# Sign bits of a split-float projection in four matmul passes a half instead of six (attention stage of a fused attention, routing and MLP kernel)

## Chip, cores and metric

One core of one Trainium2 chip. The metric is the device time of one launch in microseconds (us). The kernel before takes 763.55 us, the median of 3 runs (763.53 to 763.69).

## The reference

Three stages in a row. The change sits in the first.

```python
def _attn_ref(q, k, v, proj):                      # q, k, v: 2 x 8 heads x 768 x 64, proj: 64 x 6
    q_bits = (np.einsum('bhsd,dk->bhsk', q, proj) > 0).astype(np.int64)
    k_bits = (np.einsum('bhsd,dk->bhsk', k, proj) > 0).astype(np.int64)
    q_bucket = np.sum(q_bits * 2 ** np.arange(6), axis=-1)
    k_bucket = np.sum(k_bits * 2 ** np.arange(6), axis=-1)
    mask = q_bucket[:, :, :, None] == k_bucket[:, :, None, :]
    scores = np.where(mask, scale * np.matmul(q, k.transpose(0, 1, 3, 2)), -1e9)
...
    return np.matmul(softmax(scores), v)
# then: the rows go to one of 8 experts each (two matmuls with a relu), scaled by the gate,
# then x @ w_in, softplus, @ w_out
```

A bit is the sign of a dot product, so it has to be computed to nearly full float precision: one bit wrong moves a row to another bucket.

## The kernel before

**Pairs, groups, iterations.** Attention works on 8 pairs m of heads. A pair has 6 groups: head j = 0, 1 by three blocks u of 256 query rows. The loop in `run` has one iteration `it` for each group; group g is scored in iteration g, and later pieces of it follow one to four iterations on. The loop ends after iteration 43; a hand-written list orders the last groups together with the routing and the first expert.

**Order by hand.** What an iteration issues stands in three strings: one for TensorE (PE), one for ScalarE (ACT), one for VectorE (DVE). For iterations from 5 on they are

```python
    ORDER = ("S0 T0 V0 T1 S1 F V1 T2 R V2", "O X1 H0 H1 X0 H2 A", "M0 L0 M1 L1 r L2 D")
```

S0 and S1 are the scores of two blocks of 128 query rows (line 260, tile `s`, of which there are two, so S0 of an iteration overwrites S0 of the one before). M is the row maximum on DVE (line 270); two small GpSimd (POOL) instructions turn it into scale `sc` and bias `nb` (lines 271, 272), and X is the exponential on ACT (line 281) that needs them. T transposes the result, H and L split it into a high and a low part (ACT line 298, DVE line 303), V multiplies by v (line 317), O, F and r finish a group (lines 323, 339, 348 to 359; the small `rc` of line 325 is POOL's). Each engine works its own list in order. POOL has no string of its own: after M1 of an iteration it also splits a part of v (`split_v`, lines 153 and 154) and carries a trickle of constants for the routing.

**R, A, D** prepare the pair that is scored next, one step i = 0 to 5 an iteration. Steps 0 to 3 transpose a half (384 columns) of q or k (line 180); ACT writes the high part `qH` or `kH` (line 192), DVE the low part `qL` or `kL` (line 201), both as float32r. Steps 4 and 5 make the bits of one half each: R is six passes of 384 columns into one PSUM tile (line 186), A is empty, D compares with 0 and subtracts 0 or 1 by row (line 217) into `bt`. In `bt` rows 0 to 11 and 32 to 43 belong to q of the two heads, rows 64 to 75 and 96 to 107 to k, each with the bit and the bit less one. After step 5 four DMAs on SyncE's (SP) queue put rows of `bt` below `qL` and `kH` in the tiles Q2 and K2 of each head (line 157). The scores' second pass, with Q2 and K2 (76 rows), needs them, and so adds a large negative number where two bits differ.

For pairs 2 to 7 step 4 runs in iterations 9, 15, 21, 27, 33, 39 and step 5 in the next one; the pair's first scores are those of iterations 12, 18, 24, 30, 36, 42. Pair 0 is prepared ahead of the loop and pair 1 in iterations 0 and 1, by other strings.

**Constants.** `pH` and `pL` are the high and low part of the projection, laid out 128 by 128 for q and for k.

The functions as they stand:

Of the kernel before, what the change touches and what calls it, by code (L numbers as in the profile page):

```python
# [7 lines left out]
F32 = mybir.dt.float32  # L8
F32R = mybir.dt.float32r
# [4 lines left out]
ALU = mybir.AluOpType  # L14
AX = mybir.AxisListType
PSUM = bass.MemoryType.PSUM
P = 128
# [5 lines left out]
class Attention:  # L23
# [55 lines left out]
    def consts(self):  # L79
# [18 lines left out]
        nc.vector.tensor_copy(self.pH, pb)  # L98
        nc.vector.tensor_tensor(self.pL, pb, self.pH.bitcast(F32), op=ALU.subtract)


    WARM = 8

# [55 lines left out]
    def prep_pe(self, m, i, ps_of=None):  # L159
        nc, S, HS = self.nc, self.S, self.HS  # L160
        if i == 0:
            own = ("qH", "qL", "kH", "kL", "bt")
            self.prep[m] = {}
            if m == 0:

                for n, nm in zip(("PH", "PL"), "qk"):
                    t = self.p_p.tile([P, 2, S], F32R, tag=n, name=nm + "HL")
                    self.prep[m].update({nm + "H": t[:, 0], nm + "L": t[:, 1]})
                self.prep[m]["bt"] = self.p_p.tile([P, S], F32R, tag="p0", name="bt0", bufs=3)
                own = ()  # L170
            self.prep[m].update({n: self.ah_p.tile([P, S], F32R, tag=n, name=n) for n in own})
            self.dup[m] = {(n, j): self.dup_ps[m % 2].tile([P, S], F32R, tag=f"{n}{j}", name=f"{n}{j}")
                           for n in ("Q1", "K1", "Q2", "K2") for j in range(2)}
        T = self.prep[m]
        ps = ps_of() if ps_of else self.ps_m.tile([P, 512], F32, tag="m", name="ps_prep")
        if i < 4:
            nm, c = "qk"[i % 2], i // 2
            src = self.raws[m][nm]
            for t in range(self.NT // 2):
                nc.tensor.transpose(ps[:, t * P:(t + 1) * P],  # L180
                                    src[:, self.NT // 2 * c + t].rearrange("p j d -> p (j d)"), self.ident)
        else:
            c = i - 4
            ops = [(w, a, nm + x) for a, nm in enumerate("qk") for w, x in ((self.pH, "H"), (self.pL, "H"), (self.pH, "L"))]
            for n, (w, a, nm) in enumerate(ops):
                nc.tensor.matmul(ps[:, :HS], w[:, a], T[nm][:, c * HS:(c + 1) * HS], start=(n == 0), stop=(n == len(ops) - 1))
        return ps

    def prep_act(self, m, i, ps):
        if i < 4:  # L190
            nm, c, HS = "qk"[i % 2], i // 2, self.HS
            self.nc.scalar.activation(self.prep[m][nm + "H"][:, c * HS:(c + 1) * HS], ps[:, :HS], AF.Copy, scale=self.SC)

    def prep_dve(self, m, i, ps):
        nc, HS, D, NB = self.nc, self.HS, self.D, self.NB
        T, d = self.prep[m], self.dup[m]
        heads = range(1 if m == 0 else 0, 2)
        if i < 4:
            nm, c = "qk"[i % 2], i // 2
            sl = slice(c * HS, (c + 1) * HS)  # L200
            nc.vector.scalar_tensor_tensor(T[nm + "L"][:, sl], ps[:, :HS], self.SC, T[nm + "H"][:, sl].bitcast(F32),
                                           op0=ALU.mult, op1=ALU.subtract)
            if c == 1:
                for j in heads:
                    r = slice(D * j, D * j + D)
                    if nm == "q":
                        self.dcopy(d["Q1", j][0:D], T["qH"][r])
                        self.dcopy(d["Q1", j][D:2 * D], T["qH"][r])
                        self.dcopy(d["Q2", j][0:D], T["qL"][r])
                    else:  # L210
                        self.dcopy(d["K1", j][0:D], T["kH"][r])
                        self.dcopy(d["K1", j][D:2 * D], T["kL"][r])
                        self.dcopy(d["K2", j][0:D], T["kH"][r])
        else:
            c = i - 4
            sl = slice(c * HS, (c + 1) * HS)
            nc.vector.tensor_scalar(T["bt"][:, sl], ps[:, :HS], 0.0, self.sp, op0=ALU.is_gt, op1=ALU.subtract)  # L217
            if c == 1:
                for j in heads:
                    self.dcopy(d["Q2", j][D:D + 2 * NB], T["bt"][32 * j:32 * j + 2 * NB])  # L220
                    self.dcopy(d["K2", j][D:D + 2 * NB], T["bt"][64 + 32 * j:64 + 32 * j + 2 * NB])

    def head0(self, i):

# [139 lines left out]
    def run(self, aside, aside_ps, end):  # L364
# [12 lines left out]
        for i in range(6):  # L377
            ps = self.prep_pe(0, i, ps_any)
# [11 lines left out]
        for it in range(end):  # L390
            m, r = divmod(it, GP)
            aside(it)
            if r == 0 and m + 2 < NPAIR:
                self.load(m + 2)
            ok = lambda g: 0 <= g < NG
            T_, V_, F_ = it - LT, it - LV, it - LF
            pieces = []

            for i in [it + 1] if it > 4 else []:
                mm, i = divmod(GP + i, GP)  # L400
                if mm < NPAIR:
                    pieces.append((mm, i))
            ss = {}

            def do(k):
                a, n = k[0], int(k[1]) if k[1:] else None
                if a == "S" and ok(it):
                    ss[n] = self.scores(it, n)
                elif a == "M" and ok(it):
                    self.rowmax(it, n, ss[n])  # L410
                elif k == "X0" and ok(it):
                    self.expo(it, 0)
                elif k == "X1" and ok(it - 1):
                    self.expo(it - 1, 1)
                elif a == "T" and ok(T_):
                    self.tpose_pe(T_, n)
                elif a == "H" and ok(T_):
                    self.tpose_hi(T_, n)
                elif a == "L" and ok(T_):
                    self.tpose_lo(T_, n)  # L420
                elif a == "V" and ok(V_):
                    self.pv(V_, n)
                elif a == "O" and ok(F_):
                    self.fin1(F_)
                elif a == "F" and ok(F_):
                    self.fin_pe(F_, ss.get(1))
                elif a == "r" and ok(F_):
                    self.fin_dve(F_)
                elif a == "R":
                    for x in pieces:  # L430
                        pp[x] = self.prep_pe(*x)
                elif a == "A":
                    for x in pieces:
                        self.prep_act(*x, pp[x])
                elif a == "D":
                    for x in pieces:
                        self.prep_dve(*x, pp[x])

                if a == "p":
                    pp[n] = self.prep_pe(1, n, ps_any)  # L440
                elif a == "a":
                    self.prep_act(1, n, pp[n])
                elif a == "d":
                    self.prep_dve(1, n, pp[n])
                if k == "S0":
                    fresh[:] = aside_ps(it, ss.get(0))
                    trickle.extend(fresh)
                if k == "M0":
                    for x in fresh[:1]:
                        next(x)  # L450
                if k in ("M1", "L1", "r", "D") and trickle:
                    if next(trickle[0], 0) == 0:
                        trickle.pop(0)
                if k == "M1":

                    for t in {0: range(4), 1: range(4, self.NT)}.get(it, ()):
                        self.split_v(0, t)
                    if it == 1:
                        self.consts_c()
                    vm, vt = divmod(it + 4, GP)  # L460
                    if 0 < vm < NPAIR:
                        self.split_v(vm, vt)
            todo = [x.split() for x in self.FIRST.get(it, self.ORDER)]
            left = {y for x in todo for y in x}
            while left:
                k = next(x for x in todo if x and not left.intersection(after.get(x[0], ())))
                do(k[0])
                left.remove(k.pop(0))
# [1184 lines left out]
```

## Time and profile before

| | |
|---|---|
| median of 3 runs | 763.55 us (763.53 to 763.69) |
| the profiled execution, its own time | 764.64 us |
| its span, first to last instruction | 762.9 us |
| PE busy | 749.3 us (98%), 4235 matmuls |
| DVE busy | 595.8 us (78%) |
| ACT busy | 521.6 us (68%) |
| POOL busy | 226.8 us (30%) |
| granted PE clock, mean | 0.997 |

The times are device microseconds. A row of the timeline begins with the start of an instruction in us from the span's start and with its duration; in square brackets stands the idle time of the engine just before it and what ended it. Durations on one engine overlap a little (the next instruction starts while the last one drains), so the cost of an instruction in a busy stretch is the distance from its start to the next start. SPq rows are DMA issues on SP's queue.

### The profile page before, as it was taken

To read this page: it belongs to the slowest core of one execution; us is meant where nothing else is said; L and a number is where in the kernel's file an instruction comes from. 1 tells how busy PE (TensorE), PEld (TensorE's weight loads), DVE (VectorE), ACT (ScalarE), POOL (GpSimd) and SP (SyncE) were. 2 spreads that over 40 slices of the span, in tenths; PEclk is the share of its full clock that TensorE was granted. 3 is DMA by queue.
4 is the path that set the end of the run, shared out by engine and by line. 5 is a ranking of instruction groups with operands and counts; after the bars stand their busy time and mean duration, and the time that the engine had idled before them with its cause. 6 is when DMAs were issued, how large, how long until landed. Compare 5 with 4: busy or idle time off the path is not lost. (4 is left out here: it accounts for less than half of the span.)

```text
span 762.9 us, 13131 instructions
## 1 busy us (share of the span) xinstructions
PE 749.3 (98%) x4235; PEld 646.7 (85%) x4236; DVE 595.8 (78%) x894; ACT 521.6 (68%) x870; POOL 226.8 (30%) x609
## 2 busy tenths in 40 slices
PE   9999999999999999999999999999999999999996
PEld 6899999999999967888888888788888888888874
DVE  6898888989888889999999998758546755764442
ACT  5887887887879859899998899456553443533330
POOL 4654544446565546313222133300000000000222
PEclk9999999999999999999999999999999999999998
DMA  8845627546480014679973652343110311100111
GB/s 207 195 114 130 167 71 162 149 101 167 135 236 33 15 49 130 207 270 351 354 271 113 208 168 84 107 133 111 56 55 5 107 55 56 56 0 1 56 56 55
DMA packets 72602, 95.29 MB, mean 125 GB/s; under 512 B 31842, under 2 KB 48226, under 8 KB 72528
## 3 DMA queue, kind: packets, MB, share of 16 engines
q1 hardware_dynamic: 65552, 83.46, 36.7%
q0 software_dynamic: 3744, 9.45, 3.4%
q10 hardware_dynamic: 3232, 1.48, 0.8%
q8 instruction: 35, 0.57, 0.3%
q14 instruction: 39, 0.32, 0.1%
HBM read 105.18 MB, written 10.76 MB: 152 GB/s over the span
## 5 line engine op out<-in xcount | busy, mean ns | idle before, releaser
L1012 DVE TENSOR_TENSOR wL<-wr,wH 128x1024 fp32r<-128x1024 f32 (+1 forms) x137 | 160.4, 1200 | 8.4 <-ACT wH L1007 8.3
L1007 ACT CAST wH<-wr 128x1024 fp32r<-128x1024 f32 (+1 forms) x144 | 141.4, 1005 | 8.1 <-PE ps_g L1081 3.2
L1327 ACT ACTIVATE ga<-ps_f 128x512 f32<-128x512 f32 x48 | 28.8, 600 | 124.7 <-PE ps_f L1319 121.0
L270 DVE TENSOR_REDUCE mx<-s 128x1 f32<-128x768 f32 x96 | 91.5, 953 | 20.1 <-PE s L339 17.8
L281 ACT ACTIVATE p<-s,nb,sc 128x768 f32<-128x768 f32 x96 | 95.9, 999 | 15.9 <-POOL nb L272 12.3
L303 DVE TENSOR_TENSOR PL<-ps_t,PH 128x512 fp32r<-128x512 f32 x144 | 98.2, 683 | 7.1 <-ACT PH L298 6.6
L1333 DVE SCALAR_TENSOR_TENSOR gg<-ps_f,ga 128x512 f32<-128x512 f32 x48 | 33.2, 692 | 89.0 <-ACT ga L1329 88.8
L298 ACT CAST PH<-ps_t 128x512 fp32r<-128x512 f32 x144 | 83.7, 588 | 15.5 <-PE ps_t L293 13.1
L260 PE MATMUL s<-K,Q 76*128 76x384 f32 (+1 forms) x384 | 88.1, 351 | 1.4 <-ACT p L281 1.4
L293 PE MATMUL ps_t<-ident,p 128*128 128x128 f32 x576 | 86.4, 273 | 0.4 <-DVE bt L217 0.2
L317 PE MATMUL ps_o<-PH,vhl 128*128 128x256 f32 x288 | 86.7, 317 | 0.0
L1367 POOL DMA_INDIRECT out_dram<-acc,oidx x12 | 11.7, 973 | 238.5 <-DVE acc L1365 234.7
L1319 PE MATMUL ps_f<-x2H,mwH 128*128 128x512 f32 x192 | 75.8, 395 | 0.4 <-DVE w L1293 0.4
L1358 PE MATMUL ps_o<-mwL,gH 128*128 128x512 f32 x192 | 75.8, 395 | 0.0
L1358 PE MATMUL ps_o<-mwH,gH 128*128 128x512 f32 x192 | 75.8, 395 | 0.0
L1319 PE MATMUL ps_f<-x2H,mwL 128*128 128x512 f32 x192 | 75.7, 394 | 0.0
L1319 PE MATMUL ps_f<-x2L,mwH 128*128 128x512 f32 x192 | 75.7, 394 | 0.0
L1358 PE MATMUL ps_o<-mwH,gL 128*128 128x512 f32 x192 | 75.7, 394 | 0.0
L293 PEld LDWEIGHTS ps_t<-ident,p 128*128 128x128 f32 x576 | 69.3, 141 | 2.7 <-DVE bt L217 0.6
L317 PE MATMUL ps_o<-PL,vhl 128*64 128x256 f32 x288 | 68.3, 280 | 0.0
L260 PEld LDWEIGHTS s<-K,Q 76*128 76x128 f32 (+1 forms) x384 | 63.3, 190 | 2.9 <-ACT p L281 2.4
L1140 POOL DMA_INDIRECT x_dram<-y,cpi x17 | 20.9, 1229 | 128.4 <-ACT y L1135 97.7
(292 smaller groups left out, 1653.3 us busy)
## 6 DMA issues: line engine op xcount, KB each, us to landing
wr<-in_moe_w_dram SPq DMA_DIRECT2D x136, 512.0 KB
wraw<-in_moe_w_in_dram SPq DMA_DIRECT2D x16, 512.0 KB
wraw<-in_moe_w_out_dram SPq DMA_DIRECT2D x16, 512.0 KB
Q<-qH SPq DMA_DIRECT2D x28, 192.0 KB
K<-kH SPq DMA_DIRECT2D x28, 192.0 KB
rawv<-in_v_dram SPq DMA_DIRECT2D x8, 384.0 KB
x_dram<-x SPq DMA_DIRECT2D x8, 384.0 KB
rawq<-in_q_dram SPq DMA_DIRECT2D x14, 192.0 KB
```

The costliest lines, as they stand in the source:

```text
L260: self.nc.tensor.matmul(s[:, h, :HS], d[l, j][:kk, ts], d[r, j][:kk, h * HS:(h + 1) * HS], start=(a == 0), stop=(a == 1))
L270: nc.vector.tensor_reduce(mx, s[:, :, :self.HS], axis=AX.XY, op=ALU.max)
L281: self.nc.scalar.activation(e["P"][ti].rearrange("p (h c) -> p h c", h=2), s[:, :, :self.HS], AF.Exp, scale=sc, bias=nb, accum_out=e["sum" ...
L293: self.nc.tensor.transpose(ps[:, kk, t], e["P"][t][:, kt * P:(kt + 1) * P], self.ident)
L298: self.nc.scalar.copy(e["PH"][:, 2 * bk:2 * bk + 2].rearrange("p k n -> p (k n)"), e["T", bk])
L303: self.nc.vector.tensor_tensor(e["PL"][:, sl].rearrange("p k n -> p (k n)"), e["T", bk], e["PH"][:, sl].rearrange("p k n -> p (k n)").bitc ...
L317: self.nc.tensor.matmul(O[:n, :2 * P], vh[:, j, kt, :n], e[nm][:, kt], start=(kt == 0 and n == P), stop=(kt == NT - 1 and n == P))
L1007: self.nc.scalar.copy(self.wt[s, c][0][:, sl], self.raw[c][:, sl])
L1012: eng.tensor_tensor(L[:, sl], self.raw[c][:, sl], H[:, sl].bitcast(F32), op=ALU.subtract)
L1319: nc.tensor.matmul(ps, w[:, 0, sl], x[:, k], start=(k == 0 and n == 0), stop=(k == self.KD - 1 and n == 2))
L1333: nc.vector.scalar_tensor_tensor(gg, ps, 0.0, a, op0=ALU.max, op1=ALU.add)
L1358: nc.tensor.matmul(self.ops[i], a[:, sl], w[:, 1], start=(k == 0 and n == 0), stop=(k == self.CH - 1 and n == 2))
```

## The change

For pairs 2 to 7 the bits are made in another way. Two new constants `pw` hold the projection. In `pw[0]` columns 0 to 63 are the high part as before (one copy of each bit, not two), and columns 64 up are the low part, negated. `pw[1]` has the high part alone. R becomes four passes a half: `qH` and `kH` with `pw[0]`, `qL` and `kL` with `pw[1]`. Rows 0 to 63 of the PSUM tile then hold high times high plus high times low of the data, and rows 64 up hold minus the product with the projection's low part. A copies rows 64 up to a new tile `lo` (64 by 384, ACT). D is two instructions: a comparison of rows 0 to 63 with `lo` into rows 0 to 63 of `bt` (the bit), and that less one into rows 64 up. Bit and bit less one then lie in different places, so four DMAs of 12 rows become eight of 6 rows. The constants are built on POOL after M1 of iteration 3. Pairs 0 and 1 keep the six passes.

```diff
+    def consts_bits(self):
+        G, D, NB, z = self.nc.gpsimd, self.D, self.NB, self.zeros
+        self.pw = [self.e_p.tile([P, 2, P], F32R, name=f"pw{i}") for i in range(2)]
+        for w in self.pw:
+            for i in range(2):
+                G.tensor_copy(w[:, i], z)
+        for i in range(2):
+            for j in range(2):
+                sl, c = slice(D * j, D * j + D), 32 * i + NB * j
+                h, l = (x[sl, i, 64 * i + 32 * j:64 * i + 32 * j + NB].bitcast(F32) for x in (self.pH, self.pL))
+                for w in self.pw:
+                    G.tensor_copy(w[sl, i, c:c + NB], h)
+                G.tensor_scalar(self.pw[0][sl, i, c + 64:c + 64 + NB], l, -1.0, None, op0=ALU.mult)
...
# prep_pe, steps 4 and 5
-            ops = [(w, a, nm + x) for a, nm in enumerate("qk") for w, x in ((self.pH, "H"), (self.pL, "H"), (self.pH, "L"))]
+            ws = ((self.pH, "H"), (self.pL, "H"), (self.pH, "L")) if m < 2 else ((self.pw[0], "H"), (self.pw[1], "L"))
+            ops = [(w, a, nm + x) for a, nm in enumerate("qk") for w, x in ws]
...
# prep_act
+        elif m > 1:
+            self.prep[m]["lo"] = self.ah_p.tile([64, self.HS], F32, tag="lo", name="lo")
+            self.nc.scalar.copy(self.prep[m]["lo"], ps[64:P, :self.HS])
...
# prep_dve, steps 4 and 5
+                nc.vector.tensor_tensor(bt[0:64, sl], ps[0:64, :HS], T["lo"], op=ALU.is_gt)
+                nc.vector.tensor_scalar(bt[64:P, sl], bt[0:64, sl].bitcast(F32), -1.0, None, op0=ALU.add)
...
+                    for nm, rows in (("Q2", (0, 64)), ("K2", (96, 32))):
+                        for n, r in enumerate(rows):
+                            self.dcopy(d[nm, j][D + NB * n:D + NB * (n + 1)], bt[r + NB * j:r + NB * (j + 1)])
...
# run, when M1 has been issued
+                    if it == 3:
+                        self.consts_bits()
```

Three places in the order of instructions. First POOL's list from `nb` of iteration 3 to `sc` of iteration 4, before:

```order
L272 TENSOR_SCALAR nb<-mx,sc 128x1
L153 CAST vhl<-rawv 128x2x64
L154 TENSOR_TENSOR vhl<-rawv,vhl 128x2x64
L525 IOTA iota_i 128x21
L528 CAST iota_s<-iota_i 128x21
L325 TENSOR_SCALAR rc<-sum 128x2
L271 TENSOR_SCALAR sc<-mx 128x1
```

and now, from the same `nb` (the `pw` pattern of three rows comes four times in all):

```order
L303 TENSOR_SCALAR nb<-mx,sc 128x1
L107 CAST pw_537<-zeros 128x128 x2
L107 CAST pw_538<-zeros 128x128 x2
L113 CAST pw_537<-pH 64x6
L113 CAST pw_538<-pH 64x6
L114 TENSOR_SCALAR pw_537<-pL 64x6
```

Sixteen instructions have come between `nb` and `split_v`, and so ahead of `rc`, `sc` and `nb` of iteration 4. In the changed kernel lines 303, 302 and 356 are the former 272, 271 and 325.

Second DVE's list around D of iteration 9, before:

```order
L303 TENSOR_TENSOR PL<-ps_t,PH 128x512
L217 TENSOR_SCALAR bt<-ps_prep,sp 128x384
L270 TENSOR_REDUCE mx<-s 128x1
L303 TENSOR_TENSOR PL<-ps_t,PH 128x512
L270 TENSOR_REDUCE mx<-s 128x1
```

and now:

```order
L334 TENSOR_TENSOR PL<-ps_t,PH 128x512
L241 TENSOR_TENSOR bt<-ps_prep,lo 64x384
L242 TENSOR_SCALAR bt<-bt 64x384
L301 TENSOR_REDUCE mx<-s 128x1
L334 TENSOR_TENSOR PL<-ps_t,PH 128x512
```

One DVE instruction has become two, the second of which reads what the first wrote; both stand ahead of M0 of the next iteration.

Third SP's queue after iteration 10, with the bits of pair 2, before:

```order
L361 DMA x_dram<-x 768x1x128
L157 DMA Q_697<-bt 12x768
L157 DMA K_699<-bt 12x768
L157 DMA Q_698<-bt 12x768
L157 DMA K_700<-bt 12x768
L143 DMA rawq<-in_q_dram 128x6x64 x2
```

and now:

```order
L392 DMA x_dram<-x 768x1x128
L172 DMA Q_715<-bt 6x768 x2
L172 DMA K_717<-bt 6x768 x2
L172 DMA Q_716<-bt 6x768 x2
L172 DMA K_718<-bt 6x768 x2
L158 DMA rawq<-in_q_dram 128x6x64 x2
```

Q_697 and K_699 were the tiles of the pair's first head; its last DMA was the second in line and is now the fourth.

## Rows read from the trace of the kernel before

**Rows 1.** Windows: PE, PEld, DVE, ACT, POOL busy, granted clock, DMA; iterations 8 and 9.

```profile
52.35:57.27 4.92, 4.92 (x41) 4.88 (x40) 4.61 (x11) 4.23 (x10) 2.37 (x9) 1.00 0.96 258
57.27:62.91 5.64, 5.64 (x44) 5.61 (x43) 4.71 (x8) 4.48 (x9) 2.71 (x11) 1.00 0.93 220
```

**Rows 2.** Timeline of PE, passes for the bits in iteration 9.

```profile
58.20 0.34 PE L186 MATMUL ps_prep<-qH,pL 128*128 128x384 f32 x1
...
58.90 0.35 PE L186 MATMUL ps_prep<-kL,pH 128*128 128x384 f32 x1
```

**Rows 3.** Timeline of DVE, from D of iteration 9 to M1 of iteration 10.

```profile
59.75 0.61 DVE L217 TENSOR_SCALAR bt<-ps_prep,sp 128x384 fp32r<-128x384 f32 x1
...
61.68 0.69 DVE L303 TENSOR_TENSOR PL<-ps_t,PH 128x512 fp32r<-128x512 f32 x1 [0.26 <-ACT PH L298]
62.91 0.96 DVE L270 TENSOR_REDUCE mx<-s 128x1 f32<-128x768 f32 x1 [0.55 <-PE s L339]
```

**Rows 4.** Timeline of ACT, after H2 of iteration 9.

```profile
59.81 0.37 ACT L323 COPY Os<-ps_o 128x256 f32<-128x256 f32 x1 [1.00 <-PE ps_o L317]
```

**Rows 5.** Groups of instructions by form (count, busy us, mean ns), and one line's durations (min/median/max).

```profile
L201 DVE SCALAR_TENSOR_TENSOR qL<-ps_prep,qH 128x384 fp32r<-128x384 f32 x14 | 7.7, 547 | 0.0
L192 ACT ACTIVATE qH<-ps_prep 128x384 fp32r<-128x384 f32 x14 | 6.9, 496 | 0.9 <-PE ps_prep L180 0.9
...
L236 DVE CAST K<-kHL x2: 353/479/605, 8.5 to 9.9; 64x384 fp32r<-64x384 f32 x2
```

**Rows 6.** Timeline of POOL, iterations 3 to 5.

```profile
31.82 0.23 POOL L271 TENSOR_SCALAR sc<-mx 128x1 f32<-128x1 f32 x1
32.15 0.27 POOL L272 TENSOR_SCALAR nb<-mx,sc 128x1 f32<-128x1 f32 x1
...
35.52 0.29 POOL L359 COPY x<-xr 128x128 f32<-128x128 f32 x1
35.75 0.19 POOL L535 COPY iota_s<-iota_s 128x2 f32<-128x2 f32 x1
35.88 0.24 POOL L525 IOTA iota_i<- 128x128 int32 x1
```

**Rows 7.** Timeline of ACT: X0 of iteration 4, and its accumulator's read.

```profile
32.45 0.99 ACT L281 ACTIVATE p<-s,nb,sc 128x768 f32<-128x768 f32 x1
33.34 0.19 ACT L281 ACTIVATION_READ_ACCUMULATOR p<-s,nb,sc 128x1 f32 x1
```

**Rows 8.** Timeline of PE: S0 of iterations 3, 5 and 12.

```profile
25.02 0.97 PE L260 MATMUL s<-K,Q 128*128 128x384 f32 x4 [0.95 <-ACT p L281]
...
34.00 0.95 PE L260 MATMUL s<-K,Q 128*128 128x384 f32 x4
...
70.11 0.87 PE L260 MATMUL s<-K,Q 128*128 128x384 f32 x4
```

**Rows 9.** Timeline of SP's queue: bits of pair 2, first and last of four; a load of v.

```profile
66.03 0.82 SPq L157 DMA_DIRECT2D Q<-bt  x1
...
68.48 0.71 SPq L157 DMA_DIRECT2D K<-bt  x1
...
80.90 0.40 SPq L144 DMA_DIRECT2D rawv<-in_v_dram  x1
```

**Rows 10.** Windows of a quarter us (last two columns DMA share and GB/s) around the fourth DMA's data.

```profile
69.75:70.00 0.25, 0.25 (x5) 0.25 (x4) 0.25 (x1) 0.25 (x1) 0.15 (x2) 1.00 0.61 98
70.00:70.25 0.25, 0.25 (x4) 0.25 (x3) 0.21 (x3) 0.25 (x2) 0.25 (x2) 1.00 0.20 49
```

**Rows 11.** Timeline of PE ahead of the loop and at its last matmul; a window after it.

```profile
8.52 0.53 PE L186 MATMUL ps_prep<-qHL,pL 128*128 128x384 f32 x1
8.84 0.53 PE L186 MATMUL ps_prep<-qHL,pH 128*128 128x384 f32 x1
...
755.21 0.40 PE L1358 MATMUL ps_o<-mwH,gL 128*128 128x512 f32 x1
...
757.50:758.00 0.50, 0.00 (x0) 0.00 (x0) 0.00 (x0) 0.00 (x0) 0.50 (x1) 0.71 0.00 0
```

More of the change, by code (lines that the diff above doesn't have):

```diff
@@ L216, in prep_dve @@
             sl = slice(c * HS, (c + 1) * HS)
-            nc.vector.tensor_scalar(T["bt"][:, sl], ps[:, :HS], 0.0, self.sp, op0=ALU.is_gt, op1=ALU.subtract)
+            bt = T["bt"]
+            if m < 2:
+                nc.vector.tensor_scalar(bt[:, sl], ps[:, :HS], 0.0, self.sp, op0=ALU.is_gt, op1=ALU.subtract)
+            else:
+                nc.vector.tensor_tensor(bt[0:64, sl], ps[0:64, :HS], T["lo"], op=ALU.is_gt)
+                nc.vector.tensor_scalar(bt[64:P, sl], bt[0:64, sl].bitcast(F32), -1.0, None, op0=ALU.add)
             if c == 1:
                 for j in heads:
-                    self.dcopy(d["Q2", j][D:D + 2 * NB], T["bt"][32 * j:32 * j + 2 * NB])
-                    self.dcopy(d["K2", j][D:D + 2 * NB], T["bt"][64 + 32 * j:64 + 32 * j + 2 * NB])
+                    if m < 2:
+                        self.dcopy(d["Q2", j][D:D + 2 * NB], bt[32 * j:32 * j + 2 * NB])
+                        self.dcopy(d["K2", j][D:D + 2 * NB], bt[64 + 32 * j:64 + 32 * j + 2 * NB])
+                        continue
+                    for nm, rows in (("Q2", (0, 64)), ("K2", (96, 32))):
+                        for n, r in enumerate(rows):
+                            self.dcopy(d[nm, j][D + NB * n:D + NB * (n + 1)], bt[r + NB * j:r + NB * (j + 1)])
     def head0(self, i):
```

## Prediction

> **What bounds the kernel now.** I read the windows first, one for each iteration of the attention loop. The reader should see in them that PE is busy for the whole of an ordinary iteration (4.92 of 4.92 us) and of one that makes bits (5.64 of 5.64), while the next engine, DVE, is busy 4.71 us in the second [rows 1]. So PE is the bound here, and what a bits iteration costs more than an ordinary one is its passes. Then I read PE's timeline inside such an iteration: the passes of 384 columns start 0.175 us apart, (58.90 - 58.20) / 4 [rows 2]. Third come the timelines of the engines that get new work, to see where they stand idle: DVE has 0.26 + 0.55 = 0.81 us between D and the next M1 [rows 3], ACT 1.00 us between H2 and the copy of `Os` [rows 4]. Last I read the two queues on which the change puts more instructions, POOL [rows 6] and SP [rows 9], and who waits for them: X0 and through it PE's next S0 [rows 7, 8], and the second score pass of a new pair.
>
> The sum is made against the profiled execution: 764.64 us, 1.74 over its span and 1.09 over the median of 763.55. All terms are shifts inside the attention loop, so I add them to either. Behind the loop everything is released by the loop's results, and a shift is passed on whole.
>
> **PE, removed.** Pairs 2 to 7 have two halves each, and each half loses two passes: 24 x 0.175 = **-4.2 us** [rows 2]. The weight loads lie beside the passes. As PE has no idle time there [rows 1], all of it is on the path, provided nothing else becomes late.
>
> **DVE, hidden.** D goes from one instruction of 0.61 us [rows 3] to two. The comparison reads PSUM and SBUF over 384 columns like the split of qL, 0.547; the subtraction is SBUF to SBUF over 64 rows, and the nearest row is the cast of 64x384, 0.353 to 0.605 [rows 5]. I take the lower, since the higher lies in the crowded start, and 0.05 for the second waiting on the first: 0.95 in all, +0.34. PE's iteration shrinks by 0.35, so DVE needs 0.69 of its 0.81 us of idle time: nothing is lost. By the upper row it needs 0.95, and 0.14 x 12 = 1.7 us would come on top.
>
> **ACT, hidden.** `lo` is at most a `qH` copy, 0.496 [rows 5], and starts when the last pass ends, in the 1.00 us that ACT now idles there [rows 4]. D stands behind r and L2 on DVE and finds `lo` ready. Behind `lo` waits `Os`, which needs PE's V2 anyway. If that cover were gone, up to 0.5 us an iteration would show.
>
> **POOL, on the path once.** The sixteen instructions that build `pw` stand ahead of `rc`, `sc` and `nb` of iteration 4. No row shows them. Nearest are a 128x128 copy (next start 0.23 later) and a 128x2 copy (0.13 later) [rows 6]. Four fills at 0.23 are 0.92, twelve small ones at 0.13 are 1.56, the four multiplications some 0.05 more each, and where one waits for POOL's own earlier result it is nearer to the 0.33 between `sc` and `nb` [rows 6], say 0.5 in all: 3.2 us. Ends: 16 x 0.13 = 2.1 and 16 x 0.33 = 5.3. Before, `sc` started at 31.82, `nb` at 32.15 and X0 at 32.45, ending with the accumulator's read at 33.53 [rows 6, 7]. S0 of iteration 5 overwrites that score tile; it began at 34.00, so the slack is 0.4 after a signal of 0.06 or so. That S0 really waits for X shows in iteration 3, where PE idled 0.95 for it [rows 8]. PE, which works in order, stands still for 3.2 - 0.4 = **+2.8 us** (1.7 to 4.9), and a PE that is full afterwards does not win it back.
>
> **SP's queue, on the path six times.** Before, the first of four DMAs was issued at 66.03 and the fourth at 68.48, 0.82 apart, and the fourth's data moved until 70.25, 1.77 behind its issue [rows 9, 10]. The new pair's first head needed the first two of them by its second score pass, two passes behind 70.11, at 70.46 [rows 8]; the margin hid them. Now the first head needs four. D of iteration 10 starts 0.35 earlier (iteration 9 is shorter) and lasts 0.34 longer, so the first issue stays at 66.03 and, if a DMA of 6 rows is issued as slowly as one of 12, the fourth lands at 70.25. PE gets there 0.70 earlier, at 69.76. It waits 0.49 us, six times: **+2.9 us**. Ends: at the spacing of a load of v, 0.40 [rows 9], the fourth lands at 69.0 and nothing is lost; with the slow subtraction it is 0.75 a pair, 4.5. I take the 12-row value, because these are the same kind of transfer with the same bytes a row. The raw loads queued behind are issued some 3 us later, with three iterations to spare.
>
> The Trainium skill (DMA: Bandwidth & Descriptors, Why a DMA increments its semaphore by 16 and not by 1) says that such a DMA runs on as many engines, up to 16, as divide its rows, and that the issuing queue writes the rest of the count itself; by that rule 6 rows use 6 engines and the issue does not shrink with the rows, so the sum stays as it is. No run here shows it yet.
>
> **Sum.** -4.2 + 2.8 + 2.9 = +1.5: 766.15 for the profiled execution, **765.1 us** for the median, 0.2% slower. What a measurement of this kernel tells from no change is about 0.2%, or 1.5 us, so this is at that edge.
>
> **Rivals.**
> *The bits land in time (not slower).* The place is SP's queue after steps 5; it decides at a spacing of 0.66 us: then the fourth DMA lands by 69.76. Against it: 12-row DMAs keep 0.82; for it: another transfer takes 0.40 [rows 9]. Then -4.2 + 2.8 = -1.4, 762.15; with POOL at its lower end 761.05. If POOL's block also were covered, -4.2: 759.35.
>
> *The clock falls in POOL's stall.* PE ran at its lower level ahead of the loop, with passes 0.32 apart instead of 0.175 [rows 11], and behind its last matmul at 755.21 the granted clock fell to 0.5 within the window from 757.50, some 2 us after that matmul's end [rows 11]. A stall of 2.8 us lies beyond that; against it, the 0.95 us of iteration 3 cost nothing of the kind. If half an iteration of 4.92 us is worked off at the low level, 1.2 GHz, the price is 2.46 x (0.32 / 0.175 - 1) = 2.0, a whole one 4.1. Forecast plus 2.0: 767.1. The skill (TensorE: Matmul & The Clock Gate, Why this matters for your kernels) warns of idle gaps between bursts of matmuls for this reason; the end of the trace agrees.
>
> *DVE becomes the bound.* With the slow subtraction the loop loses 1.7 us and the bits start later: 765.1 + 1.7 + 1.6 = 768.4. Against it speaks the 0.353 of the same form in the same trace.
>
> That the passes do not go is ruled out by the order of instructions: PE has 24 matmuls fewer.
>
> **How the numbers follow.** Forecast 0.35; clock falls, with or without waits on the bits, 0.30 (0.23 and 0.07; the second gives 764.15); bits in time and clock held 0.22; POOL covered too 0.08; DVE the bound 0.05. Slower by over 0.2% (from 765.08): half of the forecast, nearly all of the clock case with waits and of the DVE case: 0.45. Faster by over 0.2% (below 762.02): POOL covered, and two fifths of the bits in time: 0.17. Within: 0.38. The range goes from the bits in time with a somewhat shorter POOL block, 761.6, to the clock case with a longer one, 768.0, and leaves out the covered POOL block, the DVE case and the tails. The forecast's own range, from its POOL ends mostly, is 764.0 to 766.8.
>
> **What would show it.** The bits passes 0.175 apart, four a half, and bits iterations 5.3 us long: the first term. An idle of 2 to 4 us on PE ahead of S0 at about 34 us, ended by ACT p or POOL nb: the second; passes 0.32 apart behind it: the clock. At S0 of iterations 12, 18 and so on, an idle of about half a us ended by a DMA, and 6-row issues 0.8 apart: the third. If PE shows no idle there the forecast is wrong by 2.9; if DVE has no idle left ahead of M1 in iterations 10, 16 and so on, the hidden part was not hidden.

## The result and the profile after

The changed kernel takes 768.61 us (median of 4 runs, 768.02 to 769.88); the kernel before, beside it, 763.62 (763.53 to 763.85, 4 runs). The ratio is 1.0064 with a 95% interval of 1.0052 to 1.0076: slower by 0.64%, 5.0 us. The forecast was 765.1 and the range ended at 768.0. The side was right, the size was not.

| | profiled execution after |
|---|---|
| its own time, span | 768.44 us, 766.7 us |
| granted PE clock, mean | 0.997 |

The first part of its page is busy time, share of the span and number of instructions by engine:

```profile
PE 745.7 (97%) x4212; PEld 639.9 (83%) x4212; DVE 600.0 (78%) x906; ACT 526.8 (69%) x882; POOL 230.5 (30%) x625
```

PE is busy 3.6 us less than before, and the span is 3.8 us longer: what was taken from PE is there, and PE stands still for longer than that. To find where, I measured the loop from one `F` matmul to the next. **Stretch n** ends at F of iteration n; it holds R of iteration n-1 and S0 of iteration n. The table has all that changed.

| stretches | what lies in them | before | after |
|---|---|---|---|
| 5 | S0 behind POOL's new block | 4.73 | 7.64 |
| 10, 11, 16, 17, 22, 23, 28, 29, 35, 40 | bits | 5.64 or 5.65 | 5.28 to 5.40 |
| 34 | bits | 5.64 | 5.47 |
| 41 | bits, and a gather on POOL | 5.64 | 6.32 |
| 12, 18, 24, 36 | first scores of a new pair | 4.92 or 4.93 | 5.52, 5.54, 5.35, 5.52 |
| 30 | the same | 5.69 | 6.57 |
| 42 | the same | 4.61 | 5.58 |

From F of iteration 4 to F of the last group this sums to +4.11 us. The loop itself began 0.27 earlier, which is no part of the change: F of iteration 4 starts anywhere from 31.16 to 32.26 in the profiles of this study. Behind the loop the 3.84 that is left is passed on whole.

Windows of the changed kernel, one for each kind of stretch (busy PE, PEld, DVE, ACT, POOL, granted clock, DMA share, GB/s):

```profile
31.99:39.63 7.64, 4.84 (x37) 4.57 (x37) 4.59 (x8) 3.89 (x10) 5.55 (x25) 1.00 0.82 182
54.39:59.31 4.92, 4.92 (x40) 4.88 (x40) 4.45 (x11) 4.37 (x10) 2.25 (x9) 1.00 0.94 279
59.31:64.60 5.29, 5.29 (x41) 5.25 (x41) 4.91 (x10) 4.52 (x10) 2.64 (x12) 1.00 0.99 239
69.90:75.42 5.52, 5.14 (x40) 4.82 (x40) 4.94 (x9) 4.44 (x11) 3.12 (x13) 1.00 0.10 27
220.37:226.69 6.32, 5.85 (x42) 5.37 (x41) 5.00 (x10) 4.32 (x10) 4.45 (x16) 1.00 0.83 270
```

Against [rows 1], a bits stretch (the third) is shorter by the two passes and PE is still busy throughout. The first, fourth and fifth hold PE's new idle time. The waits of PE say who ended it (us in total, times, longest):

```profile
PE s L291 <- ACT p L312: 4.7, 5, 2.8
PE s L291 <- DMA K<-bt: 2.0, 5, 0.7
...
PE s L291 <- issue: 0.6, 1, 0.6
```

**Stretch 5.** PE's timeline, the line that answers to the second of [rows 8]:

```profile
33.37 0.60 PE L324 MATMUL ps_t<-ident,p 128*128 128x128 f32 x4
36.77 0.79 PE L291 MATMUL s<-K,Q 128*128 128x384 f32 x3 [2.79 <-ACT p L312]
```

And POOL's, which answers to [rows 6]:

```profile
29.74 0.26 POOL L303 TENSOR_SCALAR nb<-mx,sc 128x1 f32<-128x1 f32 x1
29.95 1.00 POOL L107 CAST pw<-zeros 128x128 fp32r<-128x128 bf16 x4
...
33.41 0.29 POOL L168 CAST vhl<-rawv 128x128 fp32r<-128x128 f32 x1
...
34.99 0.24 POOL L302 TENSOR_SCALAR sc<-mx 128x1 f32<-128x1 f32 x1
35.33 0.27 POOL L303 TENSOR_SCALAR nb<-mx,sc 128x1 f32<-128x1 f32 x1
```

The sixteen instructions take 33.41 - 29.95 = 3.46 us, and `nb` of iteration 4, X0 and PE's S0 stand behind them.

**Stretch 12.** SP's queue answers to [rows 9], and PE's timeline to the last of [rows 8]:

```profile
68.25 1.60 SPq L172 DMA_DIRECT2D Q<-bt  x2
69.90 1.37 SPq L172 DMA_DIRECT2D K<-bt  x2
71.31 1.36 SPq L172 DMA_DIRECT2D Q<-bt  x2
72.72 1.36 SPq L172 DMA_DIRECT2D K<-bt  x2
```
```profile
72.05 0.52 PE L291 MATMUL s<-K,Q 128*128 128x384 f32 x2
72.94 0.59 PE L291 MATMUL s<-K,Q 76*128 76x384 f32 x2 [0.38 <-DMA K<-bt]
```

Each SP line holds two issues. 1.65 and 1.41 us for two are 0.70 to 0.83 each, where twelve rows took 0.82 [rows 9]: six rows are issued hardly faster than twelve. The first head needs the first two lines, and the fourth issue starts at 70.61. PE could start the second ones two passes behind 72.05, at 72.40 (two times 0.175), and starts them at 72.94: 0.54 lost, of the stretch's 0.60. The 0.38 in brackets is less, since the pass before it still drains into the gap.

**Stretch 41.** POOL, ACT and PE of the changed kernel:

```profile
220.16 1.21 POOL L1028 DMA_INDIRECT xg<-x_dram,idi  x1 [0.64 <-issue]
...
222.09 0.27 POOL L303 TENSOR_SCALAR nb<-mx,sc 128x1 f32<-128x1 f32 x1
```
```profile
222.40 0.99 ACT L312 ACTIVATE p<-s,nb,sc 128x768 f32<-128x768 f32 x1 [1.95 <-POOL nb L303]
```
```profile
223.53 0.97 PE L291 MATMUL s<-K,Q 128*128 128x384 f32 x4 [0.47 <-ACT p L312]
```

In iteration 40 POOL issues the first gather of the routed rows (an indirect DMA, which fetches rows by an index list). It takes 1.21 us, with 0.64 of idle time ahead of it, and stands before `rc`, `sc` and `nb`. The gather was there before the change: it started 4.97 us behind F of iteration 39 (217.49 - 212.52) and now 5.08 (220.16 - 215.08), so POOL's side of that stretch has hardly moved. PE, with two passes less on either side of F of iteration 40, comes 0.7 earlier, and finds X0 not done.

### The profile page after: what moved, and what is told of

The parts are those of the page before. It is cut to its first block, busy times and chain, and to the rows that moved or that the text cites. A ratio compares the mean times of both kernels' runs of the same rounds, so it can differ in the third digit from the quotient of the medians.

```text
span 766.7 us, 13164 instructions
## 1 busy us (share of the span) xinstructions
PE 745.7 (97%) x4212; PEld 639.9 (83%) x4212; DVE 600.0 (78%) x906; ACT 526.8 (69%) x882; POOL 230.5 (30%) x625
## 5 line engine op out<-in xcount | busy, mean ns | idle before, releaser
L291 PE MATMUL s<-K,Q 76*128 76x384 f32 (+1 forms) x384 | 90.1, 353 | 7.6 <-ACT p L312 4.7
```

The costliest lines, as they stand in the source:

```text
L291: self.nc.tensor.matmul(s[:, h, :HS], d[l, j][:kk, ts], d[r, j][:kk, h * HS:(h + 1) * HS], start=(a == 0), stop=(a == 1))
```

## Experiments

Theories, after the result: the loss is (a) POOL's block, once, (b) the bits' wait for the fourth DMA in SP's queue, six times, (c) the gather. Rivals: that D's second instruction makes the bits late, that the clock adds to (a), and that the passes are not worth what they were taken for.

**1. POOL's block spread out.** The same sixteen instructions, four after M0 in each of iterations 5 to 8 (`consts_bits` yields after each).

```diff
+                if k == "M0" and 5 <= it < 9:
+                    for _ in range(4):
+                        next(bits, None)
...
-                    if it == 3:
-                        self.consts_bits()
```

> The change, with the sixteen POOL instructions that build pw spread over iterations 5 to 8, four each after M0, instead of all after M1 of iteration 3. Theory (three separate losses: POOL's block once, the eight DMAs at six pairs, a late X0 in iteration 40): the idle of 2.8 us ahead of S0 of iteration 5 goes, nothing takes its place, and the time is that of the change less 2.9, about 765.7 us. Rival (the stall only moves, because POOL has no free time in any iteration): pieces of about half a us show at S0 of iterations 6 to 9 and the time falls by less than 1.5, to above 767.

Measured: 765.02 us (764.65 to 765.68, 11 runs), 1.0013 times before (1.0004 to 1.0022). Stretch 5 is back at 4.73; the waits for DMA and stretches 41 and 42 are as in the changed kernel:

```profile
PE s L294 <- DMA K<-bt: 2.0, 5, 0.7
PE s L294 <- ACT p L315: 1.9, 4, 1.0
```

What follows: of PE's 4.7 us of waits on X, 2.8 were this block. It cost the median 768.61 - 765.02 = 3.6 us, though stretch 5 of the profile shows 2.9. Spread out, it costs nothing that shows. The 765.7 that I expected took the stretch's 2.9 from the median.

**2. Twelve rows again.** The bit and the bit less one get columns side by side in `pw`, so that they lie in neighbouring rows of `bt`; D's second instruction subtracts 0 or 1 by row, in place; four DMAs of 12 rows.

```diff
-                nc.vector.tensor_scalar(bt[64:P, sl], bt[0:64, sl].bitcast(F32), -1.0, None, op0=ALU.add)
+                nc.vector.tensor_scalar(bt[0:64, sl], bt[0:64, sl].bitcast(F32), self.sp[0:64], None, op0=ALU.subtract)
...
+                    for n, nm in enumerate(("Q2", "K2")):
+                        r = 32 * j + 2 * NB * n
+                        self.dcopy(d[nm, j][D:D + 2 * NB], bt[r:r + 2 * NB])
```

> The change, with bit and bit less one of a head in twelve neighbouring rows again, so that four DMAs of 12 rows do what eight of 6 did; D still has two DVE instructions on 64 rows (the second subtracts 0 or 1 by row), and POOL's block stays in iteration 3. Theory (the new pair's first scores wait because the first head needs four DMAs instead of two): the idle ended by a DMA at S0 of iterations 12, 18, 24, 30, 36 and 42 goes, the time is that of the change less 4.1, about 764.5 us. Rival (the bits themselves come late, by the copy on ACT and the second DVE instruction): the idle there stays at half or more, and the time stays above 766.5.

Measured: 766.22 us (764.63 to 766.85, 11 runs), 1.0025 times before (1.0016 to 1.0034). The waits on `bt` are gone: stretches 12, 18, 24, 36 are 4.92 to 4.93, stretch 30 is 5.78, stretch 42 is 4.67. Beside those, the changed kernel lost .60 + .61 + .42 + .60 + .79 + .91 = 3.93 us there. But stretch 5 took 9.12 instead of 7.64. PE's timeline and windows there:

```profile
36.75 0.96 PE L291 MATMUL s<-K,Q 128*128 128x384 f32 x4 [2.87 <-ACT p L312]
...
38.25 0.41 PE L348 MATMUL ps_o<-PL,vhl 128*64 128x256 f32 x1
38.47 0.41 PE L348 MATMUL ps_o<-PH,vhl 128*128 128x256 f32 x1
```
```profile
37.00:38.00 1.00, 1.00 (x9) 0.96 (x8) 0.79 (x2) 1.00 (x3) 0.86 (x5) 0.97 0.37 87
38.00:39.00 1.00, 1.00 (x7) 1.00 (x6) 0.81 (x2) 0.92 (x3) 0.08 (x1) 0.50 1.24 279
39.00:40.00 1.00, 1.00 (x6) 1.00 (x5) 0.65 (x1) 0.02 (x1) 0.42 (x2) 0.50 1.09 246
40.00:42.00 2.00, 2.00 (x12) 2.00 (x12) 0.22 (x1) 1.55 (x3) 0.00 (x0) 0.66 0.39 87
```

After an idle time of 2.87 us the granted clock goes to 0.50, which is 1.2 of 2.4 GHz, and the 256-column passes stand 0.22 apart instead of 0.117. In the changed kernel's profile the idle time was 2.79 and the clock stayed:

```profile
38.00:39.00 1.00, 1.00 (x11) 1.00 (x10) 0.82 (x2) 0.92 (x3) 0.07 (x1) 1.00 1.10 248
```

What follows: (b) is right and is worth 3.9 us in the stretches; and the clock rival is real, in some executions. The median fell by 2.4 only, and not by the 4.1 that I expected, because this profile, and by their mean clocks (0.994 to 0.996 in ten of eleven runs) most others, lost time to the clock: 1.5 us in stretch 5, and 0.15 in stretch 6 (5.07 instead of 4.92).

**3. Both.** Experiments 1 and 2 together.

> Both edits together: pw built in iterations 5 to 8, and four DMAs of 12 rows. Theory: both losses go and the 24 passes less remain: the change less 7.0, about 761.6 us, some 2 us faster than the kernel before; of the 4.2 us of the passes about 1 to 1.5 is then still lost around iterations 40 and 41. Rival (PE is not the only bound and DVE or ACT keep the old pace): no faster than the kernel before, 763.6 us, with DVE without idle time in the bits iterations.

Measured: 760.77 us (760.66 to 761.12, 5 runs), 0.9956 times before (0.9942 to 0.9969): faster than both kernels. Run a second time on another chip it took 761.20 (760.46 to 761.45), 0.9961 (0.9947 to 0.9975). The loop is 2.93 us shorter than before; stretches 34 (5.48) and 41 (6.32) keep their losses. For the second run I had written:

> The faster version once more, as it was, on the same chip as the run beside it. Both theories: 760.8 us, the sum of iterations 40 to 42 16.3 us.

**4. Only the eight DMAs.** The kernel before, six passes, with each DMA of 12 rows of pairs 2 to 7 split into two of 6.

```diff
-                    self.dcopy(d["Q2", j][D:D + 2 * NB], T["bt"][32 * j:32 * j + 2 * NB])
-                    self.dcopy(d["K2", j][D:D + 2 * NB], T["bt"][64 + 32 * j:64 + 32 * j + 2 * NB])
+                    for nm, r in (("Q2", 32 * j), ("K2", 64 + 32 * j)):
+                        for x in ((0, 2 * NB),) if m < 2 else ((0, NB), (NB, 2 * NB)):
+                            self.dcopy(d[nm, j][D + x[0]:D + x[1]], T["bt"][r + x[0]:r + x[1]])
```

> The kernel before, with nothing changed but each DMA of 12 bit rows of pairs 2 to 7 split into two of 6. Theory: the first head's fourth DMA is issued some 2.4 us after the first and PE is released about 2.35 us after that, some 0.3 us later than PE came there before: an idle ended by a DMA at S0 of the six new pairs, 0.25 to 0.45 us lost at each, 765.1 to 766.3 us. Rival (the number of DMAs does not matter by itself, only bits that are made later): no idle there, 763.6 us.

Measured: 766.68 us (765.75 to 766.87, 7 runs), 1.0030 times before (1.0019 to 1.0041). Stretches 12, 18, 24, 30, 36, 42 lose .26, .13, .06, .56, .22 and 1.21, together 2.4 us. I had expected 0.25 to 0.45 at each and at most 766.3: four pairs lose less, two lose more. PE comes to the second passes of pair 2 0.35 later behind F of iteration 10 than with four passes (8.15 us instead of 7.80), so less is lost in the first five, but not nothing: even with the long iterations of before, the fourth landing is late. Stretch 42 loses more than in the changed kernel, as PE is not held up in stretch 41 here (5.65 instead of 6.32) and comes earlier. Splitting the transfers is enough to make the wait, without the new D.

**5. Only the constants.** The kernel before, with the sixteen POOL instructions after M1 of iteration 3 and nobody using `pw`.

```diff
+    def consts_bits(self):
...
+                    if it == 3:
+                        self.consts_bits()
```

> The kernel before, with nothing added but the sixteen POOL instructions after M1 of iteration 3 (their result is not used). Theory (POOL's block stops PE for 2.8 us, and in some executions TensorE's clock falls behind the stop): an idle of 2.8 us ahead of S0 of iteration 5; 2.9 us more, 766.6 to 767.0, where the clock holds, and 1.5 us more than that where it falls, with runs of one kernel that lie in two clumps. Rival (the stop costs the same in every run, and the spread comes from the DMAs of the bits): all runs within half a us of 766.8, as narrow as those of the kernel before.

Measured: 768.19 us (767.57 to 768.31, 5 runs), 1.0054 times before (1.0040 to 1.0067). Nothing but stretch 5 differs: 9.23 instead of 4.73. PE's timeline and windows:

```profile
36.21 1.05 PE L274 MATMUL s<-K,Q 128*128 128x384 f32 x4 [2.80 <-ACT p L295]
```

```profile
36.00:37.00 1.00, 0.79 (x4) 0.78 (x5) 0.34 (x1) 1.00 (x5) 1.00 (x5) 0.97 0.88 200
37.00:38.00 1.00, 1.00 (x7) 0.94 (x5) 1.00 (x2) 0.89 (x2) 0.30 (x2) 0.50 0.78 178
...
39.00:40.00 1.00, 1.00 (x6) 1.00 (x5) 0.52 (x1) 0.14 (x1) 0.01 (x1) 0.50 0.62 140
```

PE idles 2.80 us, starts at full clock, and then works at 1.2 of 2.4 GHz for over three. The 4.50 of the stretch are 2.9 of standing still, as in the changed kernel, and 1.6 of low clock. The runs of this kernel have a mean clock of 0.994 to 0.996, but for one with 0.998, which is the shortest. The price of the low clock is the 1.5 that I expected, the two clumps are not there: the runs lie within 0.74 us around 768.2, since by their means most have the low clock.

**6. The block in two halves.** As 5, with eight instructions after M1 of iteration 3 and eight after M1 of iteration 4.

```diff
...
+                    if it in (3, 4):
+                        for _ in range(8):
+                            next(bits, None)
```

> As the run before it, but eight of the sixteen POOL instructions after M1 of iteration 3 and eight after M1 of iteration 4. Theory: two stops of PE, some 1.2 us ahead of S0 of iteration 5 and 0.5 to 1 ahead of S0 of iteration 6, about 2.0 us together (765.8), the granted clock at 1.00 in all of it, and the runs in one clump. Rival (POOL's total work decides): 2.9 us as in one block.

Measured: 765.77 us (764.78 to 765.98, 11 runs), 1.0021 times before (1.0012 to 1.0030). Stretch 5 loses 1.25, stretch 6 0.09:

```profile
34.43 0.98 PE L277 MATMUL s<-K,Q 128*128 128x384 f32 x4 [1.13 <-ACT p L298]
```

The mean clock is 0.997 to 0.999 in all runs, and in the profiled execution the idle time of 1.13 us costs little beyond itself. Two expectations failed. The second stop, ahead of S0 of iteration 6, did not come. And the runs are not in one clump: three, the profiled one (764.84) among them, took 764.8 to 765.0, and eight 765.6 to 766.0. The median is 1.8 over the kernel before, while the loop of the profiled execution is 1.3 longer. The mean clock does not tell the two groups apart; what does stays open.

**7. Without D's second instruction.** Experiment 3, with the bits left undiminished in the rows that should hold the bit less one. So the mask differs, later stages work on other rows, and only the loop can be compared.

```diff
-                nc.vector.tensor_scalar(bt[0:64, sl], bt[0:64, sl].bitcast(F32), self.sp[0:64], None, op0=ALU.subtract)
```

> The faster version without D's second instruction, so the bits are not brought to bit and bit less one and the mask is another. Theory (D's length is covered by DVE's idle time in ten of twelve iterations, and the gather makes the loss in iteration 41): the bits iterations stay at 5.3 us, iteration 41 at 6.1 us or more, the time within 0.4 us of the faster version's 760.8. Rival (D's length is what PE waits for): iteration 41 falls to 5.6 or less and iteration 34 from 5.48 to 5.30, together 0.9 us, 759.9.

Measured: stretch 41 is 6.25 (6.32 in 3), stretch 34 is 5.49 (5.48), the other bits stretches 5.28 to 5.30, as in 3. The whole, 765.31 us (763.74 to 766.45), missed what I expected of it, since the work behind the loop is another. Two other stretches fell back to their lengths before the change: 30 from 5.78 to 5.69 and 42 from 4.67 to 4.61. What follows: D's length is not the cause in stretch 34, and makes 0.07 of the loss in stretch 41. On the path it is worth 0.2 us in all (0.09, 0.06 and 0.07), at three places.

**8. The gather an iteration later.** Experiment 3 with the gather in iteration 41.

```diff
-                if it == half + 12:
+                if it == half + 13:
```

> The faster version (pw built in iterations 5 to 8, four DMAs of 12 rows) with the first expert's indirect gather on POOL issued at the start of iteration 41 instead of 40. Theory (iteration 41 lasts 6.32 us because the gather stands ahead of sc and nb of iteration 40 on POOL, X0 of 40 cannot come earlier, and PE, now 0.35 earlier, waits at S0 of 41 and again at V0): iteration 41 falls to 5.3 us or little more, 1.0 us less, about 759.8 us, unless the gather then stops an ordinary iteration in the same way. Rival (the longer D makes X0 late): iteration 41 stays above 6.2 us.

Measured: 761.37 us (760.85 to 761.69, 5 runs), 0.9964 times before (0.9950 to 0.9978). Stretch 41 is 5.29, but stretch 42 is 5.61 instead of 4.67:

```profile
218.59 1.21 POOL L1033 DMA_INDIRECT xg<-x_dram,idi  x1 [0.18 <-issue]
...
220.54 0.26 POOL L306 TENSOR_SCALAR nb<-mx,sc 128x1 f32<-128x1 f32 x1
```
```profile
221.97 0.97 PE L294 MATMUL s<-K,Q 128*128 128x384 f32 x4 [0.76 <-DMA K<-bt]
```

The loss went along with the gather. The trace names a DMA for the idle time, but X0, behind this `nb`, ended at 221.91, 0.06 ahead of S0: it is the same wait under another name.

**9. The gather between `nb` of block 0 and `sc` of block 1.** Experiment 3, with the gather issued after M0 of iteration 40, so that `sc` and `nb` of X0 go first.

```diff
+                if k == "M0" and it in self.after_m0:
+                    self.after_m0[it]()
...
-                if it == half + 12:
-                    moe.gather(0)
+            att.after_m0 = {half + 12: lambda: moe.gather(0)}
```

> The faster version with the first expert's indirect gather issued on POOL after M0 of iteration 40 (behind sc and nb for X0) instead of at that iteration's start. Theory (wherever the gather stands ahead of sc and nb for X0, PE's next S0 waits for it; POOL has over a us free between M0 and M1): iteration 41 falls from 6.32 to 5.3 to 5.6 us and iteration 42 keeps 4.67, 0.7 to 1.0 us less than the faster version on the same chip, 759.8 to 760.1. Rival (there is no free place of that length on POOL): the sum of iterations 40 to 42 stays at 16.2 us or more, as in both places tried.

Measured: 760.43 us (759.94 to 760.94, 5 runs), 0.9951 times before (0.9937 to 0.9965), beside 761.20 for experiment 3 on the same chip.

```profile
214.78 0.27 POOL L306 TENSOR_SCALAR nb<-mx,sc 128x1 f32<-128x1 f32 x1
215.57 1.22 POOL L1035 DMA_INDIRECT xg<-x_dram,idi  x1 [0.53 <-issue]
216.83 0.27 POOL L305 TENSOR_SCALAR sc<-mx 128x1 f32<-128x1 f32 x1
```

Stretches 40 to 42 take 15.46 us instead of 16.29: 0.83 shorter, and the medians are 0.77 apart, though their ranges overlap. So (c) is shown by the stretches, to about 0.8 us. This is the fastest version of the study, 3.6 us under the kernel before.

## Why the prediction was right and wrong

The loop became 4.1 us longer where the sum had 1.5. Two steps failed, by 1.0 us each. In the term of SP's queue the mechanism was right and the size was not: the margin of one pair stood for six. In the term of PE's passes all 24 were counted as gain, and the gather's place on POOL, which turned one gain into a loss, was put at nothing because I had not read that queue there. The rest is 0.1 at POOL's block and some 0.5 of DVE's and ACT's new work, which I had as hidden.

**PE, removed: right in size, its proviso failed.** The passes are 0.175 apart, four a half, and eleven of twelve bits stretches are shorter, nine of them by 0.35, stretch 17 by 0.24 and stretch 34 by only 0.17 (both below). In stretch 41 it was "provided nothing else becomes late" that failed: the passes removed had covered POOL's gather, and 0.35 of gain became 0.68 of loss. I had gone through the queues at the places the change edits, and not at the one place where another stage already stood on the same queue. Together these are 1.3 us that the sum lacked, 1.0 of them by the gather.

**DVE, hidden: right in most iterations.** In the changed kernel, DVE's timeline from D of iteration 9:

```profile
62.39 0.54 DVE L241 TENSOR_TENSOR bt<-ps_prep,lo 64x384 fp32r<-64x384 f32 x1
62.97 0.42 DVE L242 TENSOR_SCALAR bt<-bt 64x384 fp32r<-64x384 f32 x1
63.42 0.96 DVE L301 TENSOR_REDUCE mx<-s 128x1 f32<-128x768 f32 x1
...
65.20 0.96 DVE L301 TENSOR_REDUCE mx<-s 128x1 f32<-128x768 f32 x1 [0.23 <-PE s L370]
```

The pair takes 1.03 from start to next start, where I had 0.95 (0.96 to 1.11 in all iterations but one), and 0.23 of idle time is left ahead of M1. In iteration 15 the subtraction took 0.97 instead of 0.35 to 0.51, so the pair took 1.58; DVE then had no idle time ahead of M1 of iteration 16, which was my sign that the hidden part is not hidden, and stretch 17 lost 0.11 of its gain. In experiments 3 and 7 stretch 17 has the full gain (5.28 and 5.29). With the 0.2 of experiment 7 the pair shows at four places, for 0.3 us together.

**ACT, hidden: right but for one stretch.** `lo` takes 0.48 and the copy of `Os` follows at 62.09; it answers to [rows 4] without the idle time:

```profile
61.57 0.48 ACT L211 COPY lo<-ps_prep 64x384 f32<-64x384 f32 x1
62.09 0.37 ACT L354 COPY Os<-ps_o 128x256 f32<-128x256 f32 x1
```

In stretch 34 the cover was gone. X0 starts 1.18 behind F there in both kernels (0.36 in stretch 28), because routing work on POOL (line 736, 0.60 us, is the last of it but `rc`) stands ahead of its `sc` and `nb`. So `lo` has no idle time to fall into, and X1 stands behind it:

```profile
186.59 0.48 ACT L211 COPY lo<-ps_prep 64x384 f32<-64x384 f32 x1
...
187.36 1.00 ACT L312 ACTIVATE p<-s,nb,sc 128x768 f32<-128x768 f32 x1
```

X1 starts 3.54 behind F, where it was 3.40 before, although PE comes 0.35 earlier; PE loses 0.18 at V0 and S1: S1 overwrites the score tile that X1 reads, and V0 needs H0, which stands behind X1. This is read from the trace; no run without `lo` was made.

**POOL, once: right in place and size, +2.91 for +2.8.** The block is 3.46 long and the slack 0.55, where I had 3.2 and 0.4. The rival of the clock, to which I gave 0.30, comes on top in part of the executions: the profiles of experiments 5 and 2 have it, at 1.6 us in each where I worked out 2.0, and that of after does not. By their mean clocks, three runs of after are like the profiled one (0.997) and one, the longest with 769.88, has 0.995. A mean tells it poorly, since 3 us at half clock move it by 0.002 only; how many runs of after had it stays open.

**SP's queue, six times: right mechanism, mis-sized, +3.9 for +2.9.** This is the step that failed in size. Its parts for iteration 12, counted from F of iteration 10:

| | forecast | measured |
|---|---|---|
| first DMA issued | 4.07 | 3.65 |
| fourth DMA issued | 6.52 | 6.0 |
| PE released | 8.29 | 8.34 |
| PE would have come | 7.80 | 7.80 |
| lost | 0.49 | 0.54 |

The first issue came 0.4 earlier than I took it: in iteration 10 it stands at 68.25, when the comparison is done and the subtraction not, so q's plain bits did not wait for D's second half. The release came 2.33 behind the fourth issue, where I had put 1.77, the end of the data of a 12-row DMA [rows 10]. The two errors nearly cancelled, so that 0.54 beside 0.49 is luck in good part. The data itself is not late:

```profile
69.50:69.75 0.25, 0.25 (x4) 0.25 (x3) 0.25 (x2) 0.25 (x1) 0.00 (x0) 1.00 0.21 49
...
71.00:71.25 0.25, 0.25 (x4) 0.25 (x3) 0.25 (x1) 0.25 (x1) 0.00 (x0) 1.00 0.21 49
...
71.75:72.00 0.25, 0.25 (x4) 0.25 (x3) 0.25 (x2) 0.25 (x2) 0.15 (x2) 1.00 0.21 49
...
72.25:72.50 0.25, 0.25 (x2) 0.00 (x0) 0.25 (x2) 0.25 (x2) 0.18 (x1) 1.00 0.04 12
72.50:72.75 0.25, 0.07 (x1) 0.00 (x0) 0.25 (x1) 0.25 (x2) 0.24 (x1) 1.00 0.20 49
```

The bursts begin in the windows from 69.50, 70.25, 71.00, 71.75 and 72.50, about as far apart as the issues; the first belongs to the issue at 68.25, so the one from 71.75 is the fourth and that from 72.50 the fifth. The fourth begins 1.1 to 1.4 behind its issue, twelve rows did so 1.3 to 1.5 behind [rows 10], and it is over by 72.50. PE's pass starts at 72.94. So what the term lacked is the time from the end of the data to PE's start, some 0.4 us: I had let PE start when the data ended. The traces' semaphore events (the last one of a transfer tells that all its data has landed) agree: the last signal of the fourth transfer came at 72.70, 2.09 behind its issue, and that of the fourth 12-row transfer before the change 2.24 behind. Six rows do not land later than twelve; the first head's last transfer is issued later, as fourth and not as second.

Then, the six pairs are not alike: 0.42 to 0.61 at four of them, 0.79 at stretch 30, where D starts 3.43 behind F and not 3.08 (as it did before the change), and 0.91 at stretch 42, where D comes late behind the gather (4.22). Experiment 4 loses most at the same two (0.56 and 1.21). I had taken one pair's margin for all six.

**The rule on rows and issue.** The Trainium skill (DMA: Bandwidth & Descriptors, Why a DMA increments its semaphore by 16 and not by 1) says on how many engines a transfer runs, and that the issuing queue writes the rest of the count at once. The trace agrees: the semaphore of a 6-row transfer is raised in seven steps, the first 1.1 to 1.2 behind the issue and ahead of the data, and that of a 12-row transfer in thirteen. That section of the Trainium skill says nothing of how long an issue takes; that six rows are issued no faster was my own step from it, and the 0.70 to 0.83 us beside 0.82 bear it out nearly.

**The rivals.** That the bits land in time is refuted by the DMA waits, that POOL is covered by the 2.79, that DVE becomes the bound by its idle 0.23, iterations 15 and 16 apart.

**The sum, put right.** -4.2 + 0.3 (stretches 17 and 34) + 1.0 (stretch 41) + 2.9 (POOL) + 3.9 (DMA) + 0.2 (new-pair stretches without DMA waits: 0.09 + 0.06) = +4.1, as the loop shows. The median's +5.0 is 0.9 more. Beside the experiments the kernel before has medians of 764.13 (23 runs), 763.94 (21) and 764.02 (9), some 0.4 over the 763.62 of four runs that the +5.0 is counted from, so up to half of the 0.9 may be those four. The profiled execution of before was 1.09 over its own median and its loop began the latest of all here; whether the rest is such a shift of the start or the clock in some runs was not told apart. By the same terms experiment 1 should stand at +1.2 (measured +0.9), experiment 2 at +0.2, and with its clock at +1.8 (+2.1), experiment 3 at -2.7 (-3.4 and -2.8), experiment 9 at about -3.5 (-3.6). They meet to 0.7 us, less than the 1.1 by which the start of the loop varies. Why the subtraction took 0.97 in iteration 15 stays open.

## What to carry to other kernels

An engine that is full hides the waits of others; before taking work from it, look at each place where another queue is only just in time, above all where a later stage has put a long instruction (here a gather) ahead of a small one on the path. Work that is needed once and long after is spread over the idle places of its queue, not put as one block ahead of a small instruction that others wait for; and a layout that keeps what travels together in neighbouring rows was worth 3.9 us here, nearly all that 24 passes were. Take a margin from every repetition of a pattern, not from the first.

## What was not expected of the hardware

- The granted clock after a stop of 2.8 to 2.9 us is not the same in each execution: it fell to 0.50 in the profiles of experiments 5 (idle 2.80) and 2 (2.87) and stayed at 1.00 in that of after (2.79). What tells them apart stays open. After 1.13 us (experiment 6) no run's mean is under 0.997.
- Between the issue of the last 6-row transfer that PE needs and PE's start lay 2.33 us at the first of the six pairs and 2.13 to 2.33 over all six. At the first the data was over by 1.9 and the last signal came at 2.09; so the end of the data in the windows is not yet the end of the wait.
- An indirect gather holds POOL for 1.21 us, with 0.18 to 0.64 of idle time ahead of it, and moves whatever stands behind it on that queue.
